# Priorities from eight forward and backward passes of the planner, and the copies of units 2 and 3 moved from ScalarE to transfers

## The chip, the core and the metric

The kernel runs on one core of a Trainium2 chip. The core has five engines that each work through their own instruction stream in order: TensorE (PE for its matmuls, PEld for its weight loads), VectorE (DVE), ScalarE (ACT), GpSimd (POOL) and SyncE (SP). SP and POOL issue transfers, which run on the core's 16 DMA engines. The metric is the device time of one execution in microseconds; lower is better.

## What is computed

The reference is a recurrent attention followed by two feed-forward layers. Everything is float32.

```
for t in range(768):                                   # batch 4, 8 heads, head size 48
    cur = einsum('bhd,bhe->bhde', u * k[t], v[t])
    y[t] = einsum('bhd,bhde->bhe', r[t], state + cur)
    state = w[t][..., None] * state + einsum('bhd,bhe->bhde', k[t], v[t])
x = y.transpose(0, 2, 1, 3).reshape(3072, 384)
x = ((x @ w_a) * (x @ w_b)) @ w_out                    # d_ff = 1536
h = x @ w_in                                           # d_ff = 2048
out = (max(h, 0) + alpha * min(h, 0)) @ w_out2
```

## The kernel before, in words

**The attention** is cut into 12 units (`unit`, L403): six chunks of 128 time steps, each in two halves of the batch, so that unit u + 2 takes the state that unit u leaves. A unit loads r, k and w twice, transposed (`Tp`, one buffer) and natural (`N`), and v. On DVE it forms the products near the diagonal (`natural`, tiles `e`, `A`), which go through DRAM (`mb`) into the matrix `M` (`diag`, L580). A tree of six multiplications on `Tp` (`tree`, L587) gives the decayed r and k; between its levels PE forms blocks (`level`, tile `psl`) that ACT copies into `M` (L647). At the end of the tree the decayed r is copied into `M` for each of two heads (`rcopy`, L658, an ACT copy at L665). k is transposed (`psk`, `kn`), the state increment is multiplied out (`dstate`, `psd`), and `state` (L713) runs twice per unit, for the chunk halves cc = 0 and 1: it copies the state `St` into `Z` for both heads (L725 on ACT), multiplies `St` by the decay and adds `psd`. `yout` multiplies `M` and `Z` (`psx`, 128 matmuls at L774, two times 64 per unit and half) and leaves `x`.

**The first layer** (`mlp1`) works on six blocks of 512 rows, each made of two units, in 12 steps: nine matmuls for `pa`, nine for `pb`, and nine into the accumulators `acc` (float32 is split into a high and a low part, hence three products). Each step needs ACT and DVE to empty PSUM (`a`, `g`). **The second layer** (`mlp2`) does the same with 16 steps for each of six blocks (`hp`, `hb`, `acd`). Weights come in as 64-bit words (`load_w`, L337): POOL issues the load, four ACT and two DVE instructions turn each weight into its two parts. POOL issues the load of a weight after the sixth weight before it is expanded. 36 weights belong to the first layer and all are expanded in the first block's stretch.

**The order of the work** is made by a planner that runs when the program is built. Every task is recorded by `Tasks.add` with an engine, a duration, a priority, what it reads and writes. `Tasks.run` (L138) plays the tasks through a model: at every moment each engine takes the ready task with the lowest priority value, transfers go through `Queues`, and the order in which tasks started becomes the order of the instruction streams. Priorities are set by hand, from a due time of each block: a unit's tasks at `pr(x)` inside a stretch, a PSUM-emptying task at its step's time minus 50, a weight 20 ahead of its step:

```
start.append(start[-1] + max(35 * len(BLOCKS[j]) + 15 * nu, 45 * nu, 100 if j == 0 else 0))
a = lo + (hi - lo) * i / len(us) - ahead
add("DVE", dve(n), p - 50, mul, r=[pb, a], w=[a])
```

Until block 0 of the first layer starts, PE runs filler matmuls (`warm`, L1081) between the first two units.

Of the kernel before, what the change touches and what calls it, by code (L numbers as in the profile page):

```python
# [34 lines left out]
class Queues:  # L35
# [5 lines left out]
        self.rings, self.open, self.n, self.t = {}, set(), 0, 0.0  # L41

    def issue(self, key, ring, now, nbytes, packet, kind):
        rate = 255e3 if kind == "slow" else 400e3
        cost = nbytes / packet / 16 * (0.009 + packet * 16 / rate)
        self.open.add(self.n)
        self.rings.setdefault(ring, []).append(
            [key, now + (1.0 if ring == "Pool" else 0.4), cost, self.n, kind, min(max(packet, 256), 6144)])
        self.n += 1

    def next(self, until):

        while until > self.t:
            heads = [q[0] for q in self.rings.values() if q]
            act = [x for x in heads if x[1] <= self.t + 1e-9 and not (x[4] == "last" and min(self.open) < x[3])]
            later = [x[1] for x in heads if x[1] > self.t + 1e-9]
            if not act:
                if not later or min(later) > until:
                    return None
                self.t = min(later)  # L60
                continue
            share = sum(x[5] for x in act) / (0.87 if len(act) == 1 and act[0][5] > 300 else 1.0)
            end = min([self.t + min(x[2] / x[5] for x in act) * share, until] + later)
            for x in act:
                x[2] -= (end - self.t) * x[5] / share
            self.t = end
            for q in self.rings.values():
                if q and q[0] in act and q[0][2] <= 1e-6:
                    x = q.pop(0)
                    self.open.discard(x[3])  # L70
                    return end + 1.1, x[0]
        return None


class Tasks:
# [59 lines left out]
            self.late[i] = late  # L135
        return i

    def run(self):  # L138
        import heapq

        t = self.t
# [22 lines left out]
        left = n  # L164
        serial = 0
        runs = []

        for i in range(n):
            if not need[i]:
                ready.setdefault(t[i][0], []).append((t[i][2], i))  # L170

        def warming():
            return self.fill and self.fill[2] <= now < self.fill[3] and start[self.fill[4]] is None
# [19 lines left out]
        def soon(eng, p, dur):  # L193
            c, at_ = {}, {}
            for i, end in ends.items():
                for s in succ[i]:
                    if t[s][0] == eng and t[s][2] < p - 4.0:
                        c[s] = c.get(s, 0) + 1
                        at_[s] = max(at_.get(s, 0.0), end + (self.LAT[t[i][0]] if t[i][0] != eng else self.SAME.get(eng, 0.0)))
            return any(c[s] == need[s] and at_[s] < now + min(0.5, dur) for s in c)  # L200

        while left:
            progress = True
            while progress:
                progress = False
                for eng, q in ready.items():
                    if busy.get(eng, 0.0) > now + 1e-9 or not q:
                        continue
                    q.sort()
                    for k, (p, i) in enumerate(q):  # L210
                        if at[i] > now + 1e-9:
                            continue
                        if eng == "PE" and warming() and low(now + t[i][1], self.work.get(i, 0.0)):
                            filler()
                            progress = True
                            break
                        if now < 75.0 and eng in ("ACT", "DVE") and soon(eng, p, t[i][1]):
                            break
                        al = t[i][5]
                        if al:  # L220
                            tag = al[0]
                            if free[tag] <= 0 or tag not in self.ANY and self.pool_seq[tag][nxt[tag]] != i:
                                continue
                            free[tag] -= 1
                            nxt[tag] += 1
                        q.pop(k)
                        if eng == "PE":
                            runs.append((now, now + t[i][1], self.work.get(i, 0.0) / max(t[i][1], 0.01)))
                        start[i] = now
                        order.append(i)  # L230
                        if t[i][6]:
                            busy[eng] = now + t[i][1]
                            end = None
                            queues.issue(i, eng, busy[eng], *self.dma[i])
                        else:
                            busy[eng] = end = now + t[i][1]
                        serial += 1
                        heapq.heappush(ev, (busy[eng], serial, -1))
                        if end is not None:
                            serial += 1  # L240
                            heapq.heappush(ev, (end, serial, i))
                        if end is not None:
                            ends[i] = end
                        progress = True
                        break
            if warming() and busy.get("PE", 0.0) <= now + 1e-9:
                filler()
            landed = queues.next(ev[0][0] if ev else 1e9)
            if landed:
                serial += 1  # L250
                heapq.heappush(ev, (landed[0], serial, landed[1]))
                continue
            if not ev:
                raise RuntimeError("stuck")
            now, _, i = heapq.heappop(ev)
            if i >= 0:
                left -= 1
                ends.pop(i, None)
                for h in users.get(i, ()):
                    left_use[h] -= 1  # L260
                    if not left_use[h]:
                        free[self.handles[h][0]] += 1
                for s in succ[i]:
                    need[s] -= 1
                    at[s] = max(at[s], now + (
                        self.LAT[t[i][0]] + self.late.get(s, 0.0) if t[s][0] != t[i][0] else self.SAME.get(t[i][0], 0.0)))
                    if not need[s]:
                        ready.setdefault(t[s][0], []).append((t[s][2], s))
                        if at[s] > now:
                            serial += 1  # L270
                            heapq.heappush(ev, (at[s], serial, -1))
        for i in order:
            (t[i][3] if i >= 0 else self.fill[0])()
        return now


@with_exitstack
def rwkv_then_moe_kernel(
# [124 lines left out]
    def unit(u, pr):  # L403
# [183 lines left out]
        def tree(h, p):  # L587
# [14 lines left out]

            RK, Wn = ([x for y in z for x in nm(f"{T}/{y}", (0, 1))] for z in ("rk", "w"))
            add("DVE", dve(8 * CH), p, halves, r=RK + Wn, w=RK)
            add("DVE", dve(n), p, decay, r=Wn, w=Wn)

        def level(h, bs, p):

# [42 lines left out]
            for hd in range(2):  # L651
# [1 line left out]
                if both and hd:  # L653
                    add("DVE", 32 // h * dve(16 * h), p, lambda hd=hd: extract(hd), r=r, w=[mn(hd, h)])
                else:
                    add("ACT", 32 // h * act(16 * h, True), p, lambda hd=hd: extract(hd), r=r, w=[mn(hd, h)])

        def rcopy(hd, b0, bs):  # L658
            q0, q1 = 4 * bs[0], 4 * bs[-1] + 4
            dst = mt(hd)[b0:b0 + 48, :, q0:q1].rearrange("p c q t -> p q c t")  # L660
            src = cur["T", u][b0:b0 + 48, 0, q0:q1].rearrange("p q (c t) -> p q c t", c=2)
            if both and hd:
                nc.vector.tensor_copy(dst, src)
            else:
                nc.scalar.copy(dst, src)  # L665
# [19 lines left out]
        def dstate(p):  # L685
# [18 lines left out]

            for i in range(nd - 1):
                add("PE", 0.0, p, lambda: None, w=[f"psd{u}_{i}"], alloc=(pool, f"psd{u}_{i}"))
            add("PE", (1.03 if apart else 1.2) * nd, p, run, r=[kn + "/0", kn + "/1", V], w=[f"psd{u}_{i}" for i in range(nd)],
                alloc=(pool, f"psd{u}_{nd - 1}"), work=672 * nd, late=1.5 if u >= 2 else 0.0)


# [2 lines left out]
        def state(cc, bs, p):  # L713
# [5 lines left out]
            def cp(hd, b0):  # L719
                x = st if u > 1 else cur["ds", u][0]  # L720
                x, z = x[b0:b0 + 48, q0:q1], zv(cc, hd)[b0:b0 + 48, q0:q1]
                if both and hd:
                    nc.vector.tensor_copy(z, x)
                else:
                    nc.scalar.copy(z, x)  # L725
# [14 lines left out]

            if u > 1 or cc:
                for hd, b0 in ((0, 64), (1, 0)):
                    e, d = ("DVE", dve(192 * nb)) if both and hd else ("ACT", act(192 * nb, u < 2))
                    add(e, d, p, lambda hd=hd, b0=b0: cp(hd, b0), r=s if u > 1 else [f"psd{u}_0"],
                        w=[zn(cc, hd, "S")])
                if u >= NU - 2 and cc:
                    return
                if u < 4:
# [67 lines left out]
        for bs in parts_:  # L816
            for hd, b0 in ((0, 64), (1, 0)):
                e, d = ("DVE", dve(512 * len(bs), True)) if both and hd else ("ACT", act(512 * len(bs)))
                add(e, d, p, lambda hd=hd, b0=b0, bs=bs: rcopy(hd, b0, bs), r=nm(T + "/r", bs), w=[mn(hd, "R")])
        for g in range(2):  # L820
            ktrans(g, pr(0.6))
        dstate(pr(0.65))
# [261 lines left out]
    with tc.manual_schedule():  # L1084
# [53 lines left out]

        add("HOST", 0, -300, new_t1, w=["T1/new"], alloc=("x", "T1"))
        xn = units(0)  # L1140
        wlead = 20
        def weights(gens, n):
            gens = list(gens)
# [100 lines left out]
```

## Time and profile before

| | us |
|---|---|
| median of three runs | 1006.99 (1004.57 to 1007.63) |
| the profiled execution, device time | 1004.32 |
| its span, first to last instruction | 1002.6 |
| mean granted TensorE clock | 0.998 of full speed |

The span is what the rows below divide. Times in them are microseconds from its start unless marked ns. An engine's busy time says how long it had an instruction in work; what counts for the end of this kernel is the time in which PE had none, and the filler.

### The profile page before, as it was taken

The numbers are of one execution on the slowest core, as the hardware profiler recorded it, in microseconds if no ns is written. First come the engines' busy times: TensorE is split into PE (matmuls) and PEld (weight loads), VectorE is DVE, ScalarE is ACT, GpSimd is POOL, SyncE is SP. The second block draws the span as 40 slices with busy tenths as digits, with TensorE's granted clock in tenths as the row PEclk, the third lists the DMA queues.
The fourth block names the chain that finished last, engine by engine and source line by source line (L and its number), as shares of the span: only waits on it lengthen the run. The fifth ranks groups of instructions, "written<-read, shape, count | busy, mean of one in ns | idle before, by whom it ended". The sixth has DMA issues, their size and how long they took to land.

```text
span 1002.6 us, 21072 instructions
## 1 busy us (share of the span) xinstructions
PE 977.1 (97%) x8804; PEld 821.3 (82%) x8804; DVE 727.6 (73%) x1215; ACT 431.4 (43%) x931; POOL 88.9 (9%) x173
## 2 busy tenths in 40 slices
PE   7999899999999999999999999999999999999998
PEld 4568677788788887887788888898989999999997
DVE  8989978899999979997935677555464646554643
ACT  0888887535544452533448994121211122111111
POOL 1233240000100010010004321000000000000000
PEclk9999999999999999999999999999999999999999
DMA  7985653234243251416026542010100100000000
GB/s 215 235 247 155 195 157 91 83 91 127 71 119 106 50 157 22 129 43 167 2 59 205 180 150 64 1 47 17 32 32 1 32 32 1 32 1 1 32 1 32
DMA packets 78159, 85.61 MB, mean 85 GB/s; under 512 B 55600, under 2 KB 64944, under 8 KB 76784
## 3 DMA queue, kind: packets, MB, share of 16 engines
q1 hardware_dynamic: 70896, 52.81, 19.8%
q0 software_dynamic: 7168, 31.46, 9.8%
q8 instruction: 69, 1.13, 0.5%
q14 instruction: 26, 0.21, 0.1%
HBM read 73.24 MB, written 11.01 MB: 84 GB/s over the span
## 4 chain that ended last, share of the span: by engine, by line
PE 63%; DVE 22%; ACT 6%; DMA 5%; issue 2%; SPq 1%; DVEq 0%; ACTq 0%
PE acd L833 15%; PE hb L833 15%; PE hp L833 10%; PE acc L833 6%; PE pb L833 6%; PE pa L833 5%; DVE Tp L324 5%; DVE A L548 5%; DVE e L324 5%; PE warm L1081 3%; DVE N L324 2%; DVE a L324 2%; PE psl L629 2%; DVE g L324 2%; DMA N<-in_rkw_n_dram 2%
## 5 line engine op out<-in xcount | busy, mean ns | idle before, releaser
L833 PE MATMUL acd<-w,g 128*128 128x384 f32 x864 | 192.6, 335 | 0.0
L1015 ACT CAST g<-g 128x512 fp32r<-128x512 f32 x96 | 59.6, 621 | 282.2 <-PE hb L833 174.6
L833 PE MATMUL acc<-g,w 128*128 128x512 f32 x648 | 175.6, 400 | 4.0 <-ACT g L895 4.0
L833 PE MATMUL pb<-x,w 128*128 128x512 f32 x648 | 160.4, 391 | 3.2 <-DVE a L324 1.5
L833 PE MATMUL pa<-x,w 128*128 128x512 f32 x648 | 161.2, 393 | 1.3 <-DVE w L324 1.3
L833 PEld LDWEIGHTS acd<-w,g 128*128 128x128 f32 x864 | 154.2, 188 | 1.8
L833 PEld LDWEIGHTS pb<-x,w 128*128 128x128 f32 x648 | 120.7, 188 | 30.1 <-DVE a L324 2.5
L833 PEld LDWEIGHTS pa<-x,w 128*128 128x128 f32 x648 | 120.9, 188 | 28.4 <-DVE w L324 1.8
L833 PEld LDWEIGHTS acc<-g,w 128*128 128x128 f32 x648 | 119.1, 189 | 29.3 <-ACT g L895 4.8
L324 DVE TENSOR_TENSOR g<-g,g 128x512 fp32r<-128x512 f32 x96 | 66.2, 689 | 81.8 <-ACT g L1015 81.1
L324 DVE TENSOR_TENSOR Tp<-Tp 112x1024 f32<-112x1024 f32 (+2 forms) x132 | 106.9, 810 | 2.5 <-DMA Tp<-in_rkw_t_dram 1.3
L833 PE MATMUL hp<-x,w 128*128 128x512 f32 x432 | 102.9, 391 | 0.0
L833 PE MATMUL hb<-x,w 128*128 128x512 f32 x432 | 102.0, 389 | 0.0
L895 ACT CAST g<-a 128x512 fp32r<-128x512 f32 x72 | 44.5, 618 | 131.6 <-DVE a L324 124.0
L833 PEld LDWEIGHTS hb<-x,w 128*128 128x128 f32 x432 | 81.1, 188 | 16.8
L833 PEld LDWEIGHTS hp<-x,w 128*128 128x128 f32 x432 | 80.8, 188 | 16.0
L833 PE MATMUL hb<-w,g 128*128 128x384 f32 x288 | 92.5, 335 | 0.0
L548 DVE TENSOR_REDUCE A<-e 128x16 f32<-128x768 f32 (+15 forms) x148 | 86.1, 582 | 2.3
L1006 DVE TENSOR_SCALAR g<-hp,al 128x512 f32<-128x512 f32 x48 | 36.0, 750 | 63.7 <-PE hp L833 63.7
L324 DVE TENSOR_TENSOR a<-a,pb 128x512 f32<-128x512 f32 x72 | 49.1, 682 | 26.7 <-PE pb L833 25.1
L324 DVE TENSOR_TENSOR g<-a,g 128x512 fp32r<-128x512 f32 x72 | 49.5, 688 | 19.3 <-ACT g L895 19.3
L833 PEld LDWEIGHTS hb<-w,g 128*128 128x128 f32 x288 | 53.7, 188 | 0.0
(83 smaller groups left out, 1081.0 us busy)
## 6 DMA issues: line engine op xcount, KB each, us to landing
raw<-in_wt_dram POOLq DMA_DIRECT2D x68, 384.0 KB, 4.1
Tp<-in_rkw_t_dram SPq DMA_DIRECT2D x33, 448.0 KB, 5.3
N<-in_rkw_n_dram SPq DMA_DIRECT2D x10, 1152.0 KB, 7.2
x2d<-x POOLq DMA_DIRECT2D x36, 128.0 KB, 2.0
x2r<-x2d SPq DMA_DIRECT2D x36, 128.0 KB, 2.3
out_dram<-o SPq DMA_DIRECT2D x24, 192.0 KB, 1.9
V<-in_v_s_dram SPq DMA_DIRECT2D x11, 384.0 KB, 5.1
Z<-in_v_s_dram SPq DMA_DIRECT2D x44, 96.0 KB, 3.1
```

The lines of the kernel that those rows point to most:

```text
L324: nc.vector.tensor_tensor(out=out, in0=a, in1=b, op=op)
L548: nc.vector.tensor_reduce(out=v[:, :, d:d + (n - 1) * (SUB + 1) + 1:SUB + 1], in_=part(st["e"], 0, n), axis=AX.X, op=ALU.add)
L629: nc.tensor.matmul(out=st["ps"][o0:o0 + ms, cc, q, zc * i:zc * i + zc], lhsT=t[b0:b0 + 48, 1, q0 + q, t0:t0 + ms], rhs=r[b0:b0 + 48, q0 + ...
L833: nc.tensor.matmul(out=out, lhsT=lhsT, rhs=rhs, start=start, stop=stop)
L895: nc.scalar.copy(c["g", f][:, 0], c["a", f])
L1006: nc.vector.tensor_scalar(out=st["m", f], in0=st["h", f], scalar1=0.0, scalar2=al[:, f:f + 1], op0=ALU.min, op1=ALU.mult)
L1015: nc.scalar.copy(st["g", f][:, 0], st["m", f])
L1081: nc.tensor.matmul(out=warm["ps"][:, 0:512], lhsT=idt, rhs=idt.unsqueeze(1).to_broadcast([128, 4, 128]), start=True, stop=True)
```

## The change

Three things change. First, `run` becomes a loop of eight passes. Each pass plays the model forward with the present priorities (`forward`), then plays it backward from the end (`backward`): the backward pass schedules each task as late as its followers, its engine and its PSUM or SBUF slot allow. A task's new priority is its latest start so found. This holds for all tasks recorded after the first two units (`K.keep`) whose hand-set priority is above -190; the others keep theirs. The order of the pass with the earliest modelled end is the one that is issued. Second, the copies of the decayed r into `M` and of the state into `Z` are made for units 2 and 3 by transfers that SP issues, within SBUF, in place of ACT copies. Third, some constants of the model change: the rate of transfers, the landing of small transfers while others are open, and the durations of the decay, `extract`, `dstate` and the copies.

```
     def issue(...):
-        rate = 255e3 if kind == "slow" else 400e3
-        cost = nbytes / packet / 16 * (0.009 + packet * 16 / rate)
+        cost = nbytes / packet / 16 * (0.009 + packet * 16 / 400e3)
...
-                    return end + 1.1, x[0]
+                    return end + (1.1 + 2.0 * (x[5] < 300 and any(self.rings.values()))), x[0]
...
-    def run(self):
+    def forward(self, prio):
...
+    def backward(self, start, done, taken):
...
+        key = lambda i: (-done[i], -i)
...
+                    i = heapq.heappop(q)[1]
+                    end = now + t[i][1]
+                    busy[eng] = end
+                    late[i] = -end
...
+                gap = self.LAT[t[d][0]] if t[d][0] != t[i][0] else self.SAME.get(t[i][0], 0.0)
+                if t[d][6]:
+                    gap += max(0.0, done[d] - start[d] - t[d][1])
...
+    def run(self):
+        t = self.t
+        prio = [x[2] for x in t]
+        best = None
+        for k in range(8):
+            end, start, done, order, taken = self.forward(prio)
+            if best is None or end < best[0]:
+                best = end, order
+            late, span = self.backward(start, done, taken)
+            prio = [x + end if i >= self.keep and t[i][2] > -190 else t[i][2] for i, x in enumerate(late)]
+        for i in best[1]:
             (t[i][3] if i >= 0 else self.fill[0])()
...
-            add("DVE", dve(n), p, decay, r=Wn, w=Wn)
+            add("DVE", {2: 0.54, 4: 0.31, 8: 0.17, 16: 0.12, 32: 0.11}.get(h, dve(n)), p, decay, r=Wn, w=Wn)
...
-                    add("ACT", 32 // h * act(16 * h, True), p, ...)
+                    add("ACT", {4: 1.09, 8: 0.87, 16: 0.75, 32: 0.59}.get(h, 1.6), p, ...)
...
         def rcopy(hd, b0, bs):
...
-            if both and hd:
+            if u in (2, 3):
+                for c in range(2):
+                    nc.sync.dma_start(
+                        out=mt(hd)[b0:b0 + 48, c], in_=cur["T", u][b0:b0 + 48, 0, :, 64 * c:64 * c + 64])
+            elif both and hd:
                 nc.vector.tensor_copy(dst, src)
...
             def cp(hd, b0):
...
-                if both and hd:
+                if u in (2, 3):
+                    nc.sync.dma_start(out=z, in_=x)
+                elif both and hd:
...
+                    if u in (2, 3):
+                        e, d = "SP", 0.48
...
-            add("PE", (1.03 if apart else 1.2) * nd, p, run, ...)
+            add("PE", 1.16 if u > 1 else 2.1, p, run, ...)
...
         xn = units(0)
+        K.keep = len(K.t)
```

## Rows read from the trace of the kernel before

**Rows 1.** The page's first part: busy time, share of the span, instructions.
```profile
PE 977.1 (97%) x8804; PEld 821.3 (82%) x8804; DVE 727.6 (73%) x1215; ACT 431.4 (43%) x931; POOL 88.9 (9%) x173
```
**Rows 2.** Windows: stretch, length, busy PE, PEld, DVE, ACT, POOL, clock, DMA share, GB/s.
```profile
0.00:63.70 63.70, 55.55 (x924) 32.60 (x925) 56.97 (x101) 35.05 (x91) 14.77 (x29) 1.00 0.87 238
63.70:165.00 101.30, 93.38 (x1152) 74.07 (x1151) 88.13 (x155) 86.63 (x198) 29.58 (x46) 0.98 0.61 169
165.00:505.00 340.00, 334.65 (x4173) 272.60 (x4172) 312.07 (x547) 152.52 (x350) 13.68 (x27) 1.00 0.33 87
505.00:600.00 95.00, 95.00 (x539) 78.63 (x539) 53.15 (x95) 77.89 (x160) 27.63 (x67) 1.00 0.50 155
600.00:1002.60 402.60, 398.48 (x2023) 363.36 (x2021) 217.30 (x321) 79.36 (x136) 3.21 (x6) 1.00 0.07 22
```
**Rows 3.** Timeline of PE where the filler ends: the first matmuls of block 0.
```profile
63.70 2.65 PE L833 MATMUL pa<-x,w 128*128 128x512 f32 x9
```
**Rows 4.** Waits of PE from 63.7 us on: total, times, longest.
```profile
PE acc L833 <- ACT g L895: 4.0, 2, 3.0
PE psk L675 <- DVE Tp L324: 1.9, 3, 0.9
...
PE pb L833 <- DVE a L324: 1.5, 2, 1.2
```
**Rows 5.** Window of 5 us with the longest wait, columns as in rows 2.
```profile
120.00:125.00 5.00, 2.33 (x6) 1.91 (x7) 5.00 (x10) 4.06 (x9) 2.37 (x2) 0.81 0.98 264
```
**Rows 6.** Timeline: nine accumulator matmuls right after that wait, and nine undisturbed ones.
```profile
122.67 3.89 PE L833 MATMUL acc<-g,w 128*128 128x512 f32 x9 [3.04 <-ACT g L895]
...
140.39 2.21 PE L833 MATMUL acc<-g,w 128*128 128x512 f32 x9
```
**Rows 7.** Groups of ACT from 85 to 165 us: busy, mean ns, idle before.
```profile
L665 ACT COPY M<-Tp 48x1024 f32<-48x1024 f32 x4 | 4.2, 1045 | 0.0
L725 ACT COPY Z<-St 48x384 f32<-48x384 f32 x6 | 3.1, 511 | 0.1
```
**Rows 8.** Window 85 to 165 us, columns as in rows 2.
```profile
85.00:165.00 80.00, 72.41 (x953) 57.39 (x952) 67.93 (x122) 71.84 (x168) 22.81 (x38) 0.98 0.63 177
```
**Rows 9.** The page's DMA parts: a queue's packets; KB each and median us to landing.
```profile
q1 hardware_dynamic: 70896, 52.81, 19.8%
...
Z<-in_v_s_dram SPq DMA_DIRECT2D x44, 96.0 KB, 3.1
...
M<-mb SPq DMA_DIRECT2D x88, 16.0 KB, 2.2
```
**Rows 10.** Chain from 85 to 165 us: its longest piece.
```profile
118.91 9.40 DMA Z<-in_v_s_dram
```
**Rows 11.** Timeline of unit 2: tree's end, next `Tp` load, output matmuls, next tree's start.
```profile
102.39 0.18 DVE L324 TENSOR_TENSOR Tp<-Tp 112x16 f32<-112x16 f32 x1
...
104.28 1.28 SPq L446 DMA_DIRECT2D Tp<-in_rkw_t_dram  x3
...
114.70 1.99 PE L774 MATMUL psx<-M,Z 128*32 128x64 f32 x128
...
114.90 1.22 DVE L324 TENSOR_TENSOR Tp<-Tp 112x1024 f32<-112x1024 f32 x1
```
**Rows 12.** Timeline of unit 3's end: state, copy, output matmuls, `Z` loads, x, next matmuls.
```profile
156.94 0.55 DVE L324 TENSOR_TENSOR St<-St,psd 112x384 f32<-112x384 f32 x1
...
159.68 0.51 ACT L725 COPY Z<-St 48x384 f32<-48x384 f32 x1
159.98 1.99 PE L774 MATMUL psx<-M,Z 128*32 128x64 f32 x128
...
161.57 2.77 SPq L469 DMA_DIRECT2D Z<-in_v_s_dram  x4
...
164.91 0.55 DVE L324 TENSOR_TENSOR x<-psx,x 128x384 fp32r<-128x384 f32 x1
...
168.17 2.21 PE L833 MATMUL pa<-x,w 128*128 128x512 f32 x9
```

More of the change, by code (lines that the diff above doesn't have):

```diff
@@ L61, in next @@
                 continue
-            share = sum(x[5] for x in act) / (0.87 if len(act) == 1 and act[0][5] > 300 else 1.0)
+            alone = 0.62 if act[0][4] == "slow" else 0.87 if act[0][5] > 300 else 1.0
+            share = sum(x[5] for x in act) / (alone if len(act) == 1 else 1.0)
             end = min([self.t + min(x[2] / x[5] for x in act) * share, until] + later)
@@ L166, in run @@
         runs = []
+        done = [0.0] * n
+        taken = {}
         for i in range(n):
             if not need[i]:
-                ready.setdefault(t[i][0], []).append((t[i][2], i))
+                ready.setdefault(t[i][0], []).append((prio[i], i))
         def warming():
@@ L196, in soon @@
                 for s in succ[i]:
-                    if t[s][0] == eng and t[s][2] < p - 4.0:
+                    if t[s][0] == eng and prio[s] < p - 4.0:
                         c[s] = c.get(s, 0) + 1
@@ L224, in run @@
                             free[tag] -= 1
+                            taken.setdefault(tag, []).append(i)
                             nxt[tag] += 1
@@ L257, in run @@
                 left -= 1
+                done[i] = now
                 ends.pop(i, None)
@@ L267, in run @@
                     if not need[s]:
-                        ready.setdefault(t[s][0], []).append((t[s][2], s))
+                        ready.setdefault(t[s][0], []).append((prio[s], s))
                         if at[s] > now:
@@ L271, in run @@
                             heapq.heappush(ev, (at[s], serial, -1))
-        for i in order:
+        return now, start, done, order, taken
+    def backward(self, start, done, taken):
+        import heapq
+        t = self.t
+        n = len(t)
+        pred = [set() for _ in range(n)]
+        last = [0] * n
+        own = {i: h for h, (tag, xs, i) in self.handles.items()}
+        edges = [set(x[4]) for x in t]
+        for tag, xs in taken.items():
+            k = self.pool_n[tag]
+            for m in range(k, len(xs)):
+                back = own[xs[m - k]]
+                edges[xs[m]].update(j for j in self.handles[back][1] if done[j] <= start[xs[m]] + 1e-6)
+        for i in range(n):
+            edges[i].discard(i)
+            for d in edges[i]:
+                last[d] += 1
+        key = lambda i: (-done[i], -i)
+        ready, busy, ev = {}, {}, []
+        at = [0.0] * n
+        late = [0.0] * n
+        for i in range(n):
+            if not last[i]:
+                heapq.heappush(ready.setdefault(t[i][0], []), (key(i), i))
+        now, left, serial = 0.0, n, 0
+        wait = []
+        while left:
+            progress = True
+            while progress:
+                progress = False
+                for eng, q in ready.items():
+                    if busy.get(eng, 0.0) > now + 1e-9 or not q:
+                        continue
+                    i = heapq.heappop(q)[1]
+                    end = now + t[i][1]
+                    busy[eng] = end
+                    late[i] = -end
+                    heapq.heappush(ev, (end, i, 1))
+                    progress = True
+            now, i, what = heapq.heappop(ev)
+            if what == 2:
+                heapq.heappush(ready.setdefault(t[i][0], []), (key(i), i))
+                continue
+            left -= 1
+            for d in edges[i]:
+                last[d] -= 1
+                gap = self.LAT[t[d][0]] if t[d][0] != t[i][0] else self.SAME.get(t[i][0], 0.0)
+                if t[d][6]:
+                    gap += max(0.0, done[d] - start[d] - t[d][1])
+                gap += self.late.get(i, 0.0) if t[d][0] != t[i][0] else 0.0
+                at[d] = max(at[d], now + gap)
+                if not last[d]:
+                    heapq.heappush(ev, (max(at[d], now), d, 2))
+        return late, now
@@ new lines, in run @@
+    def run(self):
+        t = self.t
+        prio = [x[2] for x in t]
[6 more added lines that the diff above has]
+            prio = [x + end if i >= self.keep and t[i][2] > -190 else t[i][2] for i, x in enumerate(late)]
+            self.__dict__.setdefault("log", []).append((end, span))
+        for i in best[1]:
@@ L273, in run @@
             (t[i][3] if i >= 0 else self.fill[0])()
-        return now
+        return best[0]
 @with_exitstack
@@ L655, in level @@
                 else:
-                    add("ACT", 32 // h * act(16 * h, True), p, lambda hd=hd: extract(hd), r=r, w=[mn(hd, h)])
+                    add("ACT", {4: 1.09, 8: 0.87, 16: 0.75, 32: 0.59}.get(h, 1.6), p, lambda hd=hd: extract(hd), r=r, w=[mn(hd, h)])
         def rcopy(hd, b0, bs):
@@ L706, in dstate @@
                 add("PE", 0.0, p, lambda: None, w=[f"psd{u}_{i}"], alloc=(pool, f"psd{u}_{i}"))
-            add("PE", (1.03 if apart else 1.2) * nd, p, run, r=[kn + "/0", kn + "/1", V], w=[f"psd{u}_{i}" for i in range(nd)],
+            add("PE", 1.16 if u > 1 else 2.1, p, run, r=[kn + "/0", kn + "/1", V], w=[f"psd{u}_{i}" for i in range(nd)],
                 alloc=(pool, f"psd{u}_{nd - 1}"), work=672 * nd, late=1.5 if u >= 2 else 0.0)
@@ L742, in state @@
                 for hd, b0 in ((0, 64), (1, 0)):
-                    e, d = ("DVE", dve(192 * nb)) if both and hd else ("ACT", act(192 * nb, u < 2))
+                    e, d = ("DVE", dve(192 * nb)) if both and hd else ("ACT", act(192 * nb, True) if u < 2 else 0.52)
+                    if u in (2, 3):
+                        e, d = "SP", 0.48
                     add(e, d, p, lambda hd=hd, b0=b0: cp(hd, b0), r=s if u > 1 else [f"psd{u}_0"],
-                        w=[zn(cc, hd, "S")])
+                        w=[zn(cc, hd, "S")], nbytes=48 * 1536 if e == "SP" else 0, packet=192)
                 if u >= NU - 2 and cc:
@@ L818, in unit @@
                 e, d = ("DVE", dve(512 * len(bs), True)) if both and hd else ("ACT", act(512 * len(bs)))
-                add(e, d, p, lambda hd=hd, b0=b0, bs=bs: rcopy(hd, b0, bs), r=nm(T + "/r", bs), w=[mn(hd, "R")])
+                if u in (2, 3):
+                    e, d = "SP", 0.96
+                add(e, d, p, lambda hd=hd, b0=b0, bs=bs: rcopy(hd, b0, bs), r=nm(T + "/r", bs), w=[mn(hd, "R")],
+                    nbytes=48 * 4096 if e == "SP" else 0, packet=256)
         for g in range(2):
```

## The prediction

> **What bounds the kernel now.** I read the page's first part, then windows by stage, then what PE waited for, then the groups and the timeline of the one stretch where it waits most. PE is busy for 977.1 of 1002.6 us [rows 1], but busy is not all work: up to 63.70 us it runs the first two units and filler, and only then does the first feed-forward matmul start [rows 3]. From there to the end are 938.9 us. The windows show where PE had nothing in them: 101.30 - 93.38 = 7.92 us in block 0's stretch, 340.00 - 334.65 = 5.35 us while units 4 to 11 run beside blocks 1 to 4, nothing from 505 to 600 us, and 402.60 - 398.48 = 4.12 us in the last stretch [rows 2], all of it after the last matmul, when the last rows leave. So PE is the bound from 63.7 us on, and an order of work can win three things: the 13.27 us of gaps, whatever the gaps cost in clock, and a sooner first matmul.
>
> The waits put names to the gaps [rows 4]: `acc` for ACT's cast `g`, `pb` for DVE's product `a`, `psk` for the tree, and smaller ones that the view also lists. None is a steady rate limit; each is an engine that took another task first, or a landing that came later than planned. The longest costs more than itself: the granted clock is 0.81 of full speed in the window around it [rows 5], a mix of its two levels, 1.2 and 2.4 GHz, where PE was busy for only 2.33 of 5 us; nine accumulator matmuls took 3.89 us there against 2.21 undisturbed [rows 6], so 1.68 us more.
>
> In that stretch the engines beside PE have little room: from 85 to 165 us ACT is busy 71.84 of 80 us and DVE 67.93, and the DMA engines 0.63 of the time [rows 8].
>
> **The change part by part.**
>
> *The copies taken off ACT.* Per unit two copies into `M` at 1.045 us and four into `Z` at 0.511 us [rows 7]: 2.09 + 2.04 = 4.13 us, for two units 8.3 us. Of these 4.2 + 3.1 = 7.3 us lie between 85 and 165 us. ACT falls there from 71.84 to 64.5 of 80 us, and room of 8.2 us becomes 15.5. This is the most direct gain: the 4.0 us wait for `g`, and part of the weight waits, are ACT tasks in a full queue.
>
> *The transfers put in.* `M` takes two per head, four per unit, each 48 rows of 8 runs of 256 B (384 packets, 96 KB); `Z` takes four per unit, 384 packets of 192 B (72 KB). That is 3072 packets per unit. No transfer within SBUF is in the trace. The nearest row is the load of `Z`, 96 KB in 192 B packets, 3.1 us from issue to landing; the small `M<-mb`, 16 KB, lands in 2.2 [rows 9]. These are my bounds for quiet moments, and 3.1 is the value taken, since size and packet are its own. In a crowd the same load took 9.40 us [rows 10], the upper bound. For engine time the mean of SP's queue serves: 0.198 x 16 x 1002.6 / 70896 = 45 ns per packet [rows 2, 9], so 3072 x 0.045 / 16 = 8.6 us of all 16 engines per unit, 17.3 in all. Free in 85 to 165 us are 0.37 x 80 = 29.6 us [rows 8]: it fits, but the share rises to about 0.85. The Trainium skill, "DMA: Bandwidth & Descriptors", section "Why small descriptors are slow (HBM only)", says that transfers within SBUF do not suffer the penalty of small descriptors. By that the landing would be nearer 2.2 us, and the sum below would be some 0.4 us better; no run here shows it yet.
>
> *What waits for them.* The copies into `M` are covered: in unit 2 the tree ends at 102.57 and the output matmuls start at 114.70 [rows 11], 12 us for a landing that I put at 3.1 after four issues. The second copy into `Z` is not. In unit 3 the state is ready at 156.94 + 0.55 = 157.49, ACT's last copy ends at 160.19, `psx` starts at 159.98 [rows 12]. With two issues of about 0.6 us (my estimate from the four loads of `Z` that SP issues in 2.77 us) and 3.1 us the data stand at 161.8, 1.8 us later. `x` is done at 165.46, and the next `pa` starts at 168.17 [rows 12]: 2.7 us of cover, if block 0 keeps its length. As block 0 gets shorter, that cover goes. I take 0.5 us for it, bounds 0 and 3.6 (1.8 for each unit). Behind the waiting transfers on SP stand the loads of the next unit's `Tp`, `V` and `Z`: `Tp` must not be overwritten before the copy has read it, so its r part goes out some 2 to 3 us later than at 104.28. The next tree starts at 114.90 [rows 11], over 10 us on, where a `Z` load takes 3.1; so this costs nothing, and if DVE gets ahead, what shows is the tree waiting for `Tp`; the last state update of each unit likewise waits until `Z` has been read, with a whole unit's time to spare.
>
> *The new priorities.* A latest start puts what PE needs next ahead of what it needs later, and weighs a weight, a unit's reduction and a PSUM-emptying task on one scale. Engines still take the first ready task, so no idle time is built in. Work is neither added nor removed. In block 0's stretch I take 5.5 us of the 9.6 (7.92 idle and 1.68 clock) as won, together with the freed ACT; bounds 0 and 9.6. In 165 to 505 us I take 2 of 5.35: the waits there are few and short, DVE is at 312.07 of 340 us [rows 2] and any misjudged duration moves the same kind of wait elsewhere; bounds -5 and 5.35. Up to 63.7 us the first two units keep their priorities; only the weights expanded beside them move: 0, bounds -2 and 2, as single tasks there are 0.5 to 0.6 us and three or four could change places.
>
> *The model's constants.* They cost nothing on the chip; they only decide orders, and are within the bounds above.
>
> *The sum.* -5.5 - 2.0 + 0.5 = -7.0 us against the profiled execution of 1004.32 us (span 1002.6 and 1.7 around it). The median shown is 2.67 us above that execution; the difference is carried to it: 1006.99 - 7.0 = 1000.0.
>
> **The rivals.** A measurement of this kernel can tell 0.3%, 3.0 us, from no change, so faster is below 1004.0 and slower above 1010.0.
>
> *R1, all gaps go.* Both stretches are cleaned and the start gains a little: 9.6 + 5.35 = 14.95, less 0.5, gives 992.5. For it: none of the waits is a rate limit. Against: DVE at over nine tenths beside PE, and orders fixed at build time.
>
> *R2, the transfers crowd the loads.* In the window of the longest wait the DMA share is already 0.98 [rows 5], and a load of `Z` took 9.40 us there [rows 10]. If the sixteen transfers meet weights and `Tp` in the same way, weights land late and `psx` of units 2 and 3 waits; 7.0 is given back: 1007. The Trainium skill, "Trainium Kernel Development and Optimization", section "Key Constraints", states it as a rule that transfers from SP, ACT and POOL queues run on the same 16 engines and interleave. By that rule the copies would be moved from one full resource to another. The share of 0.63 over the whole stretch [rows 8] speaks against it as the main effect.
>
> *R3, the other side: the loss of the 50 us lead of PSUM-emptying.* Before, `a` and `g` went ahead of every unit task on DVE and ACT. With latest starts they compete with reductions and tree steps, whose followers are as urgent near a unit's end. The place is DVE between 165 and 505 us. The longest such wait is 1.2 us (`pb` for `a`) [rows 4]; one in each of the ten later units is 12 us, against perhaps 5 won in block 0: 1014. It decides once six such waits in all outweigh a gain of 7. For it: DVE's 92% there. Against: the same model that makes the order charges it for each such wait, and takes the best of eight.
>
> *R4, it does little.* The first of the eight passes uses the old priorities; if no later pass ends earlier in the model, only transfers and constants change: 1006.
>
> **How the numbers follow.** Forecast 0.45 (994 to 1004), R1 0.12, R2 0.15, R3 0.20, R4 0.08. Faster: 0.45 + 0.12, 0.03 from R2 and 0.02 from R4, 0.62. Same: 0.10 from R2, 0.06 from R4, 0.02 from R3, 0.18. Slower: 0.18 from R3 and 0.02 from R2, 0.20. The range goes from 992, which leaves out the better half of R1, to 1012, which leaves out most of R3. The forecast's own range is 994 to 1004.
>
> **What would show it.** Right: in 63.7 to 165 us PE's gaps fall from 7.9 to below 4 us and the clock stays at 1.00; ACT has four copies into `M` and eight into `Z` fewer, and the transfers land in 2 to 4 us; first `pa` stands within 2 us of 63.7. R2 would show landings over 5 us and `psx` waiting for them. R3 would show `pb` or `acc` waiting for DVE `a` or ACT `g` many times after 165 us. The prediction is wrong in its step on the start if the first `pa` moves by more than 2 us, and wrong in its sum if gaps after 165 us exceed 5.4 us or a gap opens after 505 us, where now there is none.

## The result, and the profile after

| | before | after |
|---|---|---|
| median of six runs, us | 1006.72 (1004.57 to 1008.67) | 993.67 (990.57 to 995.76) |
| span of the profiled execution, us | 1002.6 | 991.4 |

The ratio is 0.9867, with a 95% interval of 0.9844 to 0.989: 13 us faster, where 7 were forecast and 992 to 1012 was the range.

The page's first part and its chain by engine, for the changed kernel (busy us, share of the span, instructions; then shares of the chain that ended last):

```profile
PE 978.1 (99%) x8808; PEld 822.5 (83%) x8808; DVE 714.5 (72%) x1215; ACT 421.6 (43%) x919; POOL 102.1 (10%) x173
...
PE 92%; DVE 2%; ACT 2%; DMA 1%; issue 1%; POOL 0%; SPq 0%; ACTq 0%; POOLq 0%; DVEq 0%
```

PE's busy time is that of before, 977.1 us [rows 1]; what went is time without work. The windows of the changed kernel, with the columns of [rows 2]:

```profile
0.00:64.00 64.00, 57.53 (x927) 33.45 (x928) 57.25 (x100) 34.21 (x90) 15.54 (x27) 1.00 0.87 231
64.00:165.00 101.00, 98.82 (x1182) 80.27 (x1181) 95.76 (x169) 83.53 (x195) 41.71 (x50) 0.98 0.73 190
165.00:505.00 340.00, 339.14 (x4251) 275.92 (x4250) 304.15 (x537) 153.56 (x348) 13.20 (x24) 1.00 0.34 89
505.00:600.00 95.00, 95.00 (x480) 78.47 (x479) 61.39 (x109) 82.07 (x171) 29.70 (x70) 1.00 0.51 155
600.00:991.40 391.40, 387.62 (x1975) 354.34 (x1973) 195.95 (x303) 68.25 (x118) 1.92 (x4) 1.00 0.06 21
```

Gaps in block 0's stretch fell from 7.92 to 2.18 us, from 165 to 505 us from 5.35 to 0.86; together 10.2 us of the 11.2 between the two spans. The first feed-forward matmul stands at 64.07 in place of 63.70, the tail is 3.78 in place of 4.12. The windows from the first `pa` to the end, before and after:

```profile
63.70:1002.60 938.90, 921.51 (x7882) 788.65 (x7880) 670.65 (x1115) 396.40 (x841) 74.11 (x146) 1.00 0.26 75
```
```profile
64.07:991.40 927.33, 920.52 (x7882) 788.98 (x7880) 657.18 (x1116) 387.35 (x830) 86.52 (x146) 1.00 0.28 78
```

The same 7882 matmuls take 921.51 and 920.52 us, so the gaps and the tail account for 10.6 of the 11.6 us won there. The two profiled executions stand 11.2 us apart, the medians 13.05; the other 1.9 us lie in no profile. DVE tells how: in block 0's stretch it is busy for 95.76 of 101 us, against 88.13 of 101.30 [rows 2]. It has the same 1215 instructions in both kernels, and does more of them sooner, 169 in that stretch in place of 155. All that PE waits for after its start, in the view of waits (total, times, longest):

```profile
PE pa L919 <- ACT a L970: 2.2, 1, 2.2
PE psl L704 <- issue: 0.9, 2, 0.5
```

Of the groups in [rows 4], and of the smaller ones in the view that they are from, none is left. The new wait of 2.2 us has its origin in a transfer. Three views of the changed kernel: the chain from 95 to 120 us, a window of 5 us (columns as above), and the timeline.

```profile
101.33 10.53 DMA raw<-in_wt_dram
```
```profile
110.00:115.00 5.00, 2.88 (x13) 2.06 (x11) 3.29 (x6) 3.56 (x9) 1.93 (x3) 1.00 1.09 329
115.00:120.00 5.00, 4.94 (x15) 3.87 (x15) 4.88 (x8) 3.81 (x9) 2.26 (x4) 0.66 1.02 381
```
```profile
111.94 0.66 ACT L437 ACTIVATE ws<-raw 128x384 f16<-128x384 f32 x1 [1.40 <-DMA raw<-in_wt_dram]
112.16 1.23 DVE L399 TENSOR_TENSOR Tp<-Tp 112x1024 f32<-112x1024 f32 x1 [1.71 <-DMA Tp<-in_rkw_t_dram]
...
114.43 0.59 ACT L970 COPY a<-pa 128x512 f32<-128x512 f32 x1
...
115.06 3.04 PE L919 MATMUL pa<-x,w 128*128 128x512 f32 x9 [2.18 <-ACT a L970]
```

A weight took 10.53 us to arrive while the DMA share stood at 1.02 to 1.09. ACT, in order, held the emptying of `pa` behind that weight's expansion, and PE stood; the granted clock was 0.66 in the window after. A late weight in a crowd is what R2 describes, at one place; that the new copies made it late, and not the loads beside them, is not shown. In a second profile of this kernel (e9) the same wait is there with 1.5 us.

### The profile page after: what moved, and what is told of

It is laid out like the page before. It is cut to its first block, busy times and chain, and to the rows that moved or that the text cites. A ratio compares the mean times of both kernels' runs of the same rounds, so it can differ in the third digit from the quotient of the medians.

```text
span 991.4 us, 21159 instructions
## 1 busy us (share of the span) xinstructions
PE 978.1 (99%) x8808; PEld 822.5 (83%) x8808; DVE 714.5 (72%) x1215; ACT 421.6 (43%) x919; POOL 102.1 (10%) x173
## 4 chain that ended last, share of the span: by engine, by line
PE 92%; DVE 2%; ACT 2%; DMA 1%; issue 1%; POOL 0%; SPq 0%; ACTq 0%; POOLq 0%; DVEq 0%
PE acd L919 15%; PE hb L919 15%; PE acc L919 15%; PE pa L919 14%; PE pb L919 14%; PE hp L919 10%; PE psl L704 3%; PE warm L1167 3%; PE psx L857 2%; PE psd L778 1%; DMA raw<-in_wt_dram 1%; PE psk L754 1%; ACT M L722 1%; DVE e L399 1%; DMA idt<-in_ident_dram 0%
## 5 line engine op out<-in xcount | busy, mean ns | idle before, releaser
L399 DVE TENSOR_TENSOR g<-g,g 128x512 fp32r<-128x512 f32 x96 | 64.2, 687 | 18.4 <-ACT g L1101 17.6
L970 ACT COPY a<-pa 128x512 f32<-128x512 f32 x72 | 41.9, 582 | 62.1 <-PE pa L919 56.9
```

The lines of the kernel that those rows point to most:

```text
L399: nc.vector.tensor_tensor(out=out, in0=a, in1=b, op=op)
L970: nc.scalar.copy(c["a", f], c["pa"])
```

## The experiments

What is given as measured is a median, its ratio to the kernel before on the same chip, and the interval of that ratio. The ratio is not the quotient of two medians; where the two differ, the text goes by the ratio. The experiments are e1 to e12 in their order here. Gaps are those of PE in the windows 64 to 165 and 165 to 505 us, of one profiled execution each. Those of e6, e10 and e11 are the slowest of their kernel's runs (1003.66, 996.85 and 1000.23 us).

**The parts, one by one.** In the first kernel the four tests for units 2 and 3 are emptied:

```
-            if u in (2, 3):
+            if u in ():
```

> The changed kernel with its eight passes and its new constants, but all copies of units 2 and 3 on ACT as before. Three theories share the 13 us between 1006.7 and 993.7 differently. P (the priorities found by the passes close the gaps): 994 to 997, gaps of PE from 64 to 505 us below 4 us. A (ACT's freed 8.3 us does it): 1001 to 1004, with waits for ACT's g and for weights back between 105 and 155 us. C (the corrected constants make the plan fit the chip): 995 to 998, so this run alone does not part C from P.

Measured: 992.51 us, 0.9876 (0.9839 to 0.9914). Two windows of its profile:

```profile
64.00:165.00 101.00, 97.83 (x1183) 78.90 (x1182) 95.91 (x169) 90.50 (x207) 39.79 (x46) 1.00 0.62 175
165.00:505.00 340.00, 338.78 (x4311) 276.07 (x4310) 305.40 (x539) 155.69 (x351) 15.00 (x27) 1.00 0.33 90
```

ACT has all its copies back and is busy for 90.50 of 101 us, more than before the change, and PE's gaps are 3.17 and 1.22 us, just over the 4 us in all that P allowed; the time is below the ranges of all three theories. Theory A falls: a fuller ACT is no obstacle if its order is right. The second kernel has one pass in place of eight, and so the hand-set priorities, with the transfers:

```
-        for k in range(8):
+        for k in range(1):
```

> The changed kernel with one pass instead of eight: hand-set priorities, new constants, transfers for units 2 and 3. P: 1002 to 1006, gaps of PE after 64 us still 10 us or more. A: 995 to 997, with the gaps of block 0's stretch gone and those from 165 to 505 us left. C: 995 to 998, with gaps gone in both stretches.

Measured: 998.47 us, 0.994 (0.9918 to 0.9962).

```profile
64.00:165.00 101.00, 94.65 (x1163) 75.30 (x1162) 93.35 (x164) 82.82 (x194) 29.91 (x49) 1.00 0.69 185
165.00:505.00 340.00, 335.84 (x4183) 274.40 (x4182) 308.99 (x541) 154.13 (x350) 13.70 (x27) 1.00 0.33 89
```

The gaps are 6.35 and 4.16 us. The time is below what P allowed and just outside what C did; A's picture, gaps gone in block 0's stretch alone, is not there. The third has both edits, so that only the constants are new.

> Hand-set priorities, one pass, no transfers: only the constants of the model are new. P and A: 1004 to 1008, as before. C: 997 to 1000, with waits from 165 to 505 us below 2 us.

Measured: 996.05 us, 0.9923 (0.9877 to 0.997).

```profile
64.00:165.00 101.00, 96.86 (x1173) 77.16 (x1172) 94.81 (x166) 89.04 (x205) 37.36 (x48) 1.00 0.61 174
165.00:505.00 340.00, 336.20 (x4237) 273.60 (x4238) 307.60 (x540) 153.15 (x349) 13.68 (x27) 1.00 0.33 90
```

With the priorities of before and the copies of before, the corrected constants alone bring some 8 us: gaps of 4.14 and 3.80 us, the clock at 1.00, DVE at 94.81 us. Of the three theories C comes nearest: the time is 1 us below its 997 to 1000, while its waits below 2 us in the later stretch were missed (the gaps there are 3.80 us). In the first run, with eight passes, they are 1.22 us; but the same kernel run again (e10) has 2.95, so what the passes do there is within what one kernel's profiles differ by.

The fourth lets the passes set the first two units' priorities as well:

```
-        K.keep = len(K.t)
+        K.keep = 0
```

> The changed kernel, but the passes also set the priorities of the first two units (all tasks above -190). If the time up to the first feed-forward matmul, about 64 us, is an order problem like the gaps were, that matmul comes 1 to 3 us sooner and the time falls to 990 to 993. If it is bound by the first loads and DVE's work on the first two units, it stays at 993 to 995.

Measured: 994.41 us, 0.989 (0.9848 to 0.9932). The first `pa` is at 65.6 us, not sooner. Its gaps are as small (2.27 and 1.64 us), so nothing is won.

**Which constants.** From here the kernels are that of before (in the code of after, one pass, no transfers) with a part of the constants, and one with the passes and none of them. One small constant stays new in all of them, and in e8 and e11: the ACT copy of the state into `Z`, 0.52 us in place of 0.41.

```
+            add("PE", 1.16 if u > 1 else 2.1, p, run, ...)                          # e5
+            add("ACT", {4: 1.09, 8: 0.87, 16: 0.75, 32: 0.59}.get(h, 1.6), p, ...)  # e6
+            add("DVE", {2: 0.54, 4: 0.31, 8: 0.17, 16: 0.12, 32: 0.11}.get(h, dve(n)), p, decay, ...)  # e6
+                    return end + (1.1 + 2.0 * (x[5] < 300 and any(self.rings.values()))), x[0]  # e7, and its rates
```

> The kernel before with a single new constant: dstate planned at 1.16 us for units 2 to 11 (2.1 for the first two) in place of 2.4 (1.2 for the last two); the trace has 1.14 for its 64 matmuls. Theory D, that the plan's false 1.2 us of PE time per unit shifts every later task of the plan against the chip: most of the constants' 9 us come with it, 996 to 999. Theory E, that the too short extract and decay are what spoils the plan: 1004 to 1007. Theory Q, that it is the landing of transfers: 1004 to 1007.

Measured: 1002.1 us, 0.997 (0.9951 to 0.9988).

> The kernel before with only the durations of extract (ACT, 0.75 for 0.53 at h = 16) and of the decay (DVE) new. D: 1003 to 1007. E: 996 to 1000. Q: 1003 to 1007.

Measured: 999.93 us, 0.9949 (0.9931 to 0.9967).

> The kernel before with only the model of the transfers new: their rate, what a lone one gets, and 2 us more for small packets beside others. D and E: 1003 to 1007. Q: 996 to 1000, with the wait of psx for the diagonal's transfer gone.

Measured: 1007.12 us, 1.0013 (0.9997 to 1.003).

D wins 3 us, E 5, Q nothing. E's expectation was met by e6, D's by no run: e5 lies between the two ranges. The durations of both kinds count. By what they were off is seen in the trace of before:

```profile
107.54 1.14 PE L699 MATMUL psd<-V,kn 64*48 64x48 f32 x64
```
```profile
L647 ACT COPY M<-psl 16x256 f32<-16x256 f32 x42 | 15.3, 363 | 4.6 <-PE psl L629 4.2
L324 DVE TENSOR_TENSOR Tp<-Tp 112x256 f32<-112x256 f32 x11 | 7.0, 638 | 0.1
```

The 64 `dstate` matmuls take 1.14 us and were planned at 2.4. Two such ACT copies make one `extract`, 0.73 us, planned at 0.53. The decay at h = 2 takes 0.64 us and was planned at 0.33. The profile tells where each run left its time. The gaps from 165 to 505 us, for e5, e6 and e7 in turn:

```profile
165.00:505.00 340.00, 338.31 (x4191) 275.14 (x4190) 314.53 (x551) 157.41 (x358) 13.84 (x27) 1.00 0.33 89
```
```profile
165.00:505.00 340.00, 337.50 (x4207) 275.24 (x4196) 315.64 (x553) 157.77 (x359) 13.68 (x27) 1.00 0.33 88
```
```profile
165.00:505.00 340.00, 334.74 (x4173) 271.80 (x4171) 311.48 (x546) 153.03 (x352) 13.68 (x27) 1.00 0.32 88
```

Each duration by itself takes these gaps from 5.35 to 1.69 and 2.50 us; the model of the transfers leaves them at 5.26. But the start gives some of it back. The first matmuls of block 0 in the tile view of `pa` (ns min/median/max, then first and last start in us), for e5, e6 and e7:

```profile
L919 PE MATMUL pa<-x,w x27: 388/389/499, 68.4 to 78.5; 128*128 128x512 f32 x27
```
```profile
L919 PE MATMUL pa<-x,w x18: 387/393/792, 70.6 to 79.0; 128*128 128x512 f32 x18
```
```profile
L919 PE MATMUL pa<-x,w x25: 387/389/793, 67.8 to 79.9; 128*128 128x512 f32 x25
```

With a part of the constants the first `pa` comes at 67.8 to 70.6 us; with all of them it stands at 64.3 (e3), and with none at 63.70 [rows 3]. The span divides there into a start and a rest, and the rest holds the same feed-forward work in every kernel. In us, of the profiled executions:

| | first `pa` | from there to the end |
|---|---|---|
| before | 63.7 | 938.9 |
| e3, all constants | 64.3 | 931.3 |
| e5, `dstate` alone | 68.4 | 931.9 |
| e6, `extract` and decay alone | 70.6 | 931.3 |
| e7, transfer model alone | 67.8 | 936.3 |

In these profiles, behind the first `pa`, either kind of duration alone brings what all constants bring together. They do not add up there; what parts these runs from e3 is the later start. Now the passes on the old constants:

> Eight passes, no transfers, all constants as before. If the passes are worth the same 3.5 us whatever the constants (996.05 to 992.51 with the new ones), this gives 1001 to 1004. If passes need a true model to be of use, 1004 to 1009. If priorities alone would have closed the gaps, 993 to 997.

Measured: 1007.27 us, 1.0003 (0.9975 to 1.003).

```profile
64.00:165.00 101.00, 92.84 (x1150) 73.96 (x1149) 89.64 (x161) 88.49 (x203) 38.73 (x46) 0.98 0.61 175
165.00:505.00 340.00, 335.25 (x4148) 271.06 (x4147) 307.82 (x541) 152.36 (x346) 13.66 (x27) 1.00 0.32 88
```

Gaps of 8.16 and 4.75 us, the first `pa` at 64.3 us and 940.4 us from there: eight passes on a false model win nothing. This is the run that parts the causes: the passes' order is only as good as the durations it is played with.

**What is left of the transfers, and of more passes.** The next two are the changed kernel and the first experiment again, on one chip.

> The changed kernel once more, for a direct comparison on one chip with the next run, which differs from it by the transfers alone. If the transfers win nothing beside the new priorities, this is the same or up to 2 us slower than the next; if they win, it is 1 to 4 us faster.

Measured: 993.86 us, 0.9867 (0.9847 to 0.9886).

> Eight passes, new constants, copies of units 2 and 3 on ACT (the first experiment again). 992 to 994 if transfers win nothing; 994 to 997 if they do.

Measured: 995.23 us, 0.9879 (0.986 to 0.9897). The first experiment had stood at 0.9876. The intervals overlap almost wholly: the transfers of units 2 and 3 win or lose nothing that these runs can tell. Under the priorities set by hand they win nothing either (e2 0.994, e3 0.9923). Next, the passes with the new durations but the old model of the transfers, without the transfers:

> Eight passes, no transfers, the new durations of dstate, extract and decay, but the old model of the transfers. If the model of the transfers is of no use on the chip, as the transfer-model run suggests (1007.1), 991 to 994; if passes need it, 995 to 999.

Measured: 998.39 us, 0.991 (0.9893 to 0.9927), slower by 3 us than e10 with the new model. Two views of it, the tile view of `pa` and the windows:

```profile
L919 PE MATMUL pa<-x,w x27: 387/389/796, 67.9 to 79.2; 128*128 128x512 f32 x27
```
```profile
64.00:165.00 101.00, 98.25 (x1265) 78.48 (x1266) 94.80 (x170) 92.65 (x212) 42.20 (x48) 1.00 0.65 178
165.00:505.00 340.00, 335.85 (x4178) 273.27 (x4177) 306.52 (x540) 153.60 (x348) 13.72 (x27) 1.00 0.34 89
```

The first `pa` is at 67.9 us against 64.0 in e10; from there to the end it is 930.3 us against 931.0. So the model of the transfers, worthless beside the old durations, counts beside the true ones, and in these two profiles wholly at the start. Last, more passes:

```
-        for k in range(8):
+        for k in range(32):
```

> Eight passes made 32, no transfers. The planner's own end falls from 980.2 to 979.1 us. If the chip follows the model in such small steps, 991 to 992.5; if the rest is what the model does not know, 991 to 996, no clear difference from eight passes.

Measured: 992.85 us, 0.9862 (0.9838 to 0.9886). Not to be told from eight passes: the second reading holds. No version here beats the changed kernel by more than the measurement is uncertain.

## Why the prediction was right, and where its steps were not

**The bound.** Right. PE's work after its start is nearly the same in both kernels, 921.5 and 920.5 us, and the gaps were what could be won; 10.2 of 13.27 us were.

**The sum.** The direction and the order of size were right, -7.0 against -13.0. Block 0's stretch was put at -5.5 and gave 5.74 us of gaps; the clock there is 0.98 as before, since the new wait cost it again (0.66 in one window); in the second profile (e9) it is 1.00. The term that was mis-sized is the later one. The stretch from 165 to 505 us was put at -2.0, with a bound of -5 on the other side; it gave 4.49. The reason given there, that a misjudged duration moves the same wait elsewhere, was the point: the change corrected just those durations. The result, 993.67, is just outside the forecast's own 994 to 1004 and nearest to R1, "all gaps go", at 992.5, which had a chance of 0.12. That it lies in the wider range is in part luck. The sum had the constants at nothing, and they alone bring some 8 us (e3). It counted on the freed ACT, which brings nothing that can be told (e10), and on the new priorities, which bring nothing without the constants (e8).

**The model's constants.** This step failed. The prediction had: "They cost nothing on the chip; they only decide orders, and are within the bounds above." They decide orders, and that is worth some 8 of the 13 us without the other two parts of the change (e3), while the passes without them are worth nothing (e8).

**The new priorities.** Put at 7.5 us together with the freed ACT. By the runs they add some 5 us to the true constants without the transfers (0.9923 to 0.9876, intervals overlapping), some 7 with them (0.994 in e2 to 0.9867, intervals apart), and nothing to the false ones.

**The copies taken off ACT.** "This is the most direct gain" failed. Without the transfers ACT is busy for 90.50 of 101 us and the time is the same (e1, e10). The 4.0 us wait for `g` [rows 4] was order, not load: with all copies on ACT it is 1.0 us in e1 and 1.5 in e10, and the view of e3 has it no more.

**The transfers put in.** The price of 0.5 us is inside what cannot be told from nothing, but the landings were not as sized. The page's DMA issues of the changed kernel (KB each, median us to landing):

```profile
Z<-in_v_s_dram SPq DMA_DIRECT2D x44, 96.0 KB, 3.2
...
M<-Tp SPq DMA_DIRECT2D x8, 96.0 KB, 2.7
Z<-St SPq DMA_DIRECT2D x8, 72.0 KB, 6.4
```

The copies into `M` land in 2.7 us in the median against the 3.1 taken. The copies into `Z` take 6.4, though they are smaller, so the sign "in 2 to 4 us" failed for them. `psx` never waited for them. But the prediction gave the state update "a whole unit's time to spare" behind the copy, and in the second profile of this kernel (e9) that was used up: two copies into `Z` took 11.8 and 12.1 us, and DVE stood for one of them.

```profile
DVE St L399 <- DMA Z<-St: 1.1, 1, 1.1
```

The DMA share from 85 to 165 us rose from 0.63 [rows 8] to 0.72, not to 0.85. The Trainium skill, "DMA: Bandwidth & Descriptors", section "Why small descriptors are slow (HBM only)", says that transfers within SBUF do not suffer the penalty of small descriptors. No run here shows it: `M<-Tp` lands sooner than the load of `Z` of the same size, 2.7 against 3.2 us, but in longer packets, and `Z<-St` in the same packets lands later.

**The rivals.** R2 happened at one place, for 2.2 us and a dip of the clock, and did not decide. The Trainium skill, "Trainium Kernel Development and Optimization", section "Key Constraints", has transfers of the SP, ACT and POOL queues interleave on the same 16 engines. The trace agrees: a weight that POOL issued was 10.53 us under way, against a median of 4.5, with SP's transfers beside it at a DMA share of 1.02 to 1.09. R3 did not happen: no wait for `a` or `g` is left after 165 us, so the lead of 50 us was not needed. R4 is excluded, since one pass (e2) and eight differ; its price of 1006 was wrong too, since e2 is that very case and took 998.47 us.

**What stays open.** Which single exchanges of tasks closed the gaps was not traced, and why a partly corrected model puts the first `pa` 4 to 7 us later was only located, not explained. The order of the changed kernel with ACT doing the copies was not tried as such, since each plan is made anew. For the same reason each version was seen through one plan only, and a lucky plan is not excluded for any single run. Against luck for the whole stands that every kernel here with at least one corrected duration is faster than before, clear of its interval, and the two without (e7, e8) are not.

## What to carry to other kernels

Where a planner fixes the order of work, compare its durations with the trace before improving its search: here a few durations that were off by up to 1.3 us cost some 8 us under the priorities set by hand, and a better search on them won nothing. An engine that is busy for nine tenths beside the bound is not yet a cause; move its load and its order separately and see which one the time follows.

## What was not expected of the hardware

Two transfers within SBUF of nearly the same kind differed by more than two to one in landing, by their medians 2.7 us (96 KB, 256 B runs) and 6.4 us (72 KB, 192 B runs). They went out at different moments: windows of 20 us of the changed kernel, in which the first `M` copies (issued from 95.50 us) and the second `Z` copies (from 104.44 us) fall:

```profile
80.00:100.00 20.00, 20.00 (x263) 16.47 (x263) 19.78 (x35) 18.77 (x57) 15.21 (x15) 1.00 0.52 130
100.00:120.00 20.00, 17.82 (x131) 14.04 (x129) 18.01 (x37) 16.85 (x35) 9.59 (x14) 0.91 1.02 314
```

The DMA share was 0.52 in the one and 1.02 in the other. Taken moment by moment, the tile views show that one kind of copy differs by as much. The four `M` copies issued from 95.5 us landed in 2.5 to 2.7 us, the four from 139.9 us in 2.7 to 5.9. The two `Z` copies of 104.4 us took 12.0 and 12.2 us, those of 148.0 us 5.3 and 5.5. In e2 the two of 132.2 us, at a DMA share of 0.82, took at most 4.1. So the run of 192 B alone does not make 6.4 us, and the moment counts for more than the kind. That it is the crowd that counts at each moment fits these shares, but no run of its own varied the crowd.
